# One layer of long convolution and routed experts: routing's small operations between the large ones, PSUM banks by user, the spectrum in two layouts

## The chip, the cores and the metric

The kernel runs on one core of a Trainium2 chip. The metric is the device time of one execution in microseconds (us): 2072.83 us as the median of three runs (2069.47 to 2073.29).

The engines are written as in the profile: PE is TensorE's matmul, PEld its weight load, DVE is VectorE, ACT ScalarE, POOL GpSimd, and SP the queue that issues most DMAs.

## The reference

```python
def _attn_ref(x, v, pos_emb, w1, w2):            # x, v: 4 x 11456 x 128
    h_mlp = np.maximum(pos_emb @ w1, 0.0) @ w2
    h_filt = h_mlp * np.exp(-0.01 * np.arange(S))[:, None]
    u = x * v
    Uf, Hf = np.fft.rfft(u, n=2*S, axis=1), np.fft.rfft(h_filt, n=2*S, axis=0)
    y = np.fft.irfft(Uf * Hf[None], n=2*S, axis=1)[:, :S, :]
    return x * y
def _moe_ref(x, modality_id, w_gate, modality_bias, w1, w2):   # 45824 rows, 8 experts
    logits = x @ w_gate + modality_bias[modality_id]
    e_idx = np.argmax(logits, axis=1)            # the gate is its softmax value
    for e in range(8):
        mask = e_idx == e
        out[mask] = gate_w[mask, None] * (np.maximum(x[mask] @ w1[e], 0) @ w2[e])
```

All of it is float32. A row of the convolution's output goes to one of eight experts, and the result goes back to the row's own place.

## The kernel before

**Convolution.** The transform of a batch is done as 90 x 64: a transform over 90 by matmuls with a constant matrix, then one over 64 that is folded into the second set of matmuls. The spectrum of a batch stays in SBUF in one tile `A` of 128 x 2 x 90 x 128 floats (block, frequency, channel).

Four kinds of stages follow each other on a written time line (`Timeline`, line 151). Each stage puts functions at times. `run` sorts them by time, place, rank and index, and this order is the program order of every engine, for the tile framework reorders nothing on PE, ACT, DVE and SP. Dependencies between instructions are kept by semaphores. For PSUM they are kept by whole banks within one tensor.

- The first stage builds the filter and transforms batch 0.
- A *middle* stage (`middle_stages`, line 546) has 23 groups. A group reads four frequencies of `A` (`spectrum`, 16 PE instructions at line 625), multiplies them by the filter's spectrum on DVE (lines 634, 643 and 652 or 654) and POOL, and transforms them back into `A` (`inverse`, line 669, copied by ACT at line 673).
- An *outer* stage (`outer`, line 849) has 16 steps `t` with some more for the routing's end. Outer stages 1 to 3 finish batch `b - 1` and start batch `b` in the same tile `A`. In a step:
  - `turn` (line 690) transposes a piece of `A` on PE: 16 transposes of a 128 x 90 operand with a 128 x 128 identity, in four banks, copied by four ACT copies.
  - `inverse_stages.transform` (line 697) makes the output `py` from these copies (line 703); ACT copies one half (706), DVE adds (707), subtracts (708) and multiplies by x, which is the *gate* (709).
  - `forward_stages` multiplies x and v on DVE (480), adds (483) and subtracts (484) the halves, and transforms the product of the step before on PE (495), copied by ACT into `A` (498).
  - `route_stages` works on octets `o`, one in two steps: two `turn` halves (751), `logits` (759), `logits_turn` (766), `biased` (772), `choice` with nine DVE operations (780 to 802), `send` with three matmuls `pr` (818 to 823) and four DVE operations (825 to 829), and `store`, the DMA of the finished rows (809), for which there are three `xo` tiles.
- The last outer stage, which has no next batch, has an order of its own (`LAST`). An expert stage follows it: 90 tiles of 512 rows, and some of 256.

The table `OUTER` (line 58) gives each function's step relative to its piece. `choice:3` runs at `t = q + 3`, where only odd `q` act; `send:4` comes one step after it. So the choice of an octet and its `pr` matmuls never stand in the same step. Even steps of an outer stage hold a choice, odd steps a send.

**PSUM.** There is a pool of four one-bank tiles (`bank`, line 200), which `turn`, routing and the middle's `pw` share, and a pool of two two-bank tiles (`pair`, line 374), which the forward transform, `py` and the middle's spectrum share.

Of the kernel before, what the change touches and what calls it, by code (L numbers as in the profile page):

```python
# [12 lines left out]
F32 = mybir.dt.float32  # L13
F32R = mybir.dt.float32r
BF16 = mybir.dt.bfloat16
# [23 lines left out]
NM = (NP + 1) // 2  # L39
NQ = N2 // 4  # L40
# [55 lines left out]
def shape_constants():  # L96
# [4 lines left out]
    fwd = np.zeros((2, 64, 2, N1))  # L101
    fwd[:, :HALF, 0], fwd[:, :HALF, 1] = even, odd
# [31 lines left out]
    tri = np.concatenate([-(q >= p).astype(float), np.ones((D, D))], 1)  # L134
# [10 lines left out]
        "c_fwd": f(fwd.reshape(D, 2 * N1)),   # L145
# [29 lines left out]
for _name, _n in (("tok", NC), ("first", E * NC), ("keep", E * NC),  # L175
                  ("tri", D), ("ones", D), ("reg", E), ("iota", NF)):
    SMALL[_name] = (_at, _at + _n)
    _at += _n
# [4 lines left out]
def hyena_moe_kernel(ctx: ExitStack, tc: tile.TileContext, a: dict, out: bass.AP,  # L183
# [16 lines left out]
    def bank(name):  # L200
        return banks[-1].tile([D, 512], F32, tag="ps", name=name)
# [13 lines left out]
    both = cst.tile([D, 2 * D], BF16, name="both")  # L215
# [152 lines left out]
    with ExitStack() as cv:  # L368
        banks.append(cv.enter_context(tc.tile_pool(name="ps", bufs=4, space=PSUM)))
        pairs = cv.enter_context(tc.tile_pool(name="pp", bufs=2, space=PSUM))  # L370
        keepp = cv.enter_context(tc.tile_pool(name="keepp", bufs=1))
        U = 1024

        def pair(name):
            return pairs.tile([D, 2, 512], F32, tag="pp", name=name)
# [3 lines left out]
        fwd = keepp.tile([D, 2, N1], F32, name="fwd")  # L379
# [24 lines left out]
        def split_constants():  # L404
            dve.tensor_scalar_add(base, sm("reg"), FAR)
            dve.tensor_copy(both, small[:, SMALL["tri"][0]:SMALL["ones"][1]])
# [16 lines left out]
        flatA = A.rearrange("p b k d -> p (b k d)")  # L423
# [43 lines left out]
        def forward_stages(b):  # L467
# [9 lines left out]
            def product(q):  # L477

                u, e = kept.pop((q, "xd")), kept.pop((q, "v"))
                paced(dve.tensor_mul(u, u, e))  # L480
                e = kept[q, "e"] = e.rearrange("p (c m) -> p c m", c=2)
                u = u.rearrange("p (w m) -> p w m", w=2)
                dve.tensor_add(e[:, 0], u[:, 0], u[:, 1])
                paced(dve.tensor_sub(e[:, 1], u[:, 0], u[:, 1]))

            def transform(q):

                e = kept.pop((q, "e")).rearrange("p c (j n) -> p c j n", n=N2)
                for h in range(2):
                    p = pair("s1")  # L490
                    for j in range(4):
                        for c in range(2):
                            for blk in range(2):
                                at = slice(64 * blk, 64 * blk + 64)
                                pe.matmul(p[64 * c:64 * c + 64, blk, N1 * j:N1 * j + N1],
                                          e[at, c, 4 * h + j], fwd[at, c], start=True, stop=True)
                    d0 = 8 * q + 4 * h
                    act.copy(A[:, :, :, d0:d0 + 4],
                             p[:, :, 0:4 * N1].rearrange("p b (n k) -> p b k n", n=4))
# [766 lines left out]
```

## Time and profile before

| | before |
|---|---|
| median of three runs | 2072.83 us |
| the profiled execution's own time | 2074.09 us |
| span in its profile | 2072.3 us |
| busy PE / PEld / DVE / ACT / POOL | 94% / 75% / 85% / 62% / 56% |
| mean granted TensorE clock | 0.982 of 2.4 GHz |
| DMA | 379.46 MB, 183 GB/s on the mean |

The shares are means over stages with different limits, so the page's first part can't be read as a bound. The order in which to read is: the stages (a window for each), then the instructions of one step in order of time, engine by engine. In a time line a row is a start, a length, an engine, a line and an operation; what stands in square brackets is the idle time before it and what ended it. An instruction may start before the one ahead of it has ended.

### The profile page before, as it was taken

What the parts mean: (1) busy time and instruction counts of PE and PEld (TensorE: products, weight loads), DVE (VectorE), ACT (ScalarE), POOL (GpSimd) and SP (SyncE); (2) the same over time, 40 slices, a digit from 0 to 9 for tenths busy, and PEclk for the clock granted to TensorE, in tenths of its full rate; (3) what the DMA queues carried; (4) which work ended last, traced back from release to release, by engine and by line L of the source; (5) the groups of instructions that cost most, each with busy time, mean ns of one, the idle gap of its engine ahead of it and who ended that gap; (6) DMA issues with size and microseconds to landing.
All of it is one profiled execution on the core that took longest, in us unless ns stands there. A gap on an engine that the chain in (4) does not pass through costs nothing. (4 is left out here: it accounts for less than half of the span.)

```text
span 2072.3 us, 50243 instructions
## 1 busy us (share of the span) xinstructions
PE 1958.3 (94%) x17646; PEld 1554.1 (75%) x17646; DVE 1752.4 (85%) x2612; ACT 1284.4 (62%) x2404; POOL 1169.4 (56%) x1054
## 2 busy tenths in 40 slices
PE   8899898999989998999789999999999999999997
PEld 8688665776667665776468888877888888888897
DVE  6599899999999899996678888897888778878886
ACT  5555675457744675456456666666666666666675
POOL 0144004766678476974456678786555555555654
PEclk9999999999999999999899999999999999999998
DMA  8565688889988898856787456654645555555421
GB/s 319 184 191 173 231 280 268 268 264 314 327 270 253 280 339 288 283 183 179 199 248 205 97 127 138 133 124 103 118 97 97 97 100 98 96 98 100 86 40 29
DMA packets 610842, 379.46 MB, mean 183 GB/s; under 512 B 424026, under 2 KB 542005, under 8 KB 610585
## 3 DMA queue, kind: packets, MB, share of 16 engines
q1 hardware_dynamic: 587193, 328.61, 58.2%
q0 software_dynamic: 23104, 47.34, 6.6%
q8 instruction: 141, 2.31, 0.5%
q14 instruction: 116, 0.95, 0.2%
q10 hardware_dynamic: 288, 0.25, 0.1%
HBM read 272.74 MB, written 103.70 MB: 182 GB/s over the span
## 5 line engine op out<-in xcount | busy, mean ns | idle before, releaser
L1094 ACT ACTIVATE hh<-ph 128x512 fp32r<-128x512 f32 x724 | 434.0, 599 | 323.2 <-PE ph L1091 320.2
L1095 DVE SCALAR_TENSOR_TENSOR hl<-ph,hh 128x512 fp32r<-128x512 f32 x724 | 488.5, 680 | 164.4 <-ACT hh L1094 155.6
L276 POOL DMA_INDIRECT xs<-back,to x360 | 405.4, 1126 | 319.9 <-DVE se L797 107.9
L1160 POOL DMA_INDIRECT out<-ot,x x362 | 373.3, 1031 | 160.2 <-issue 36.7
L1089 PE MATMUL ph<-xh,wh 128*128 128x512 f32 (+1 forms) x792 | 298.0, 376 | 8.3 <-ACT wh L1060 8.3
L1091 PE MATMUL ph<-xl,wh 128*128 128x512 f32 (+1 forms) x792 | 296.2, 374 | 9.0 <-POOL xl L1077 9.0
L1115 PE MATMUL po<-hl,wh 128*128 128x512 f32 (+1 forms) x792 | 295.6, 373 | 0.9 <-DVE hl L1095 0.6
L1090 PE MATMUL ph<-xh,wl 128*128 128x512 f32 (+1 forms) x792 | 295.6, 373 | 0.0
L1113 PE MATMUL po<-hh,wh 128*128 128x512 f32 (+1 forms) x792 | 295.1, 373 | 0.2 <-ACT hh L1094 0.2
L1114 PE MATMUL po<-hh,wl 128*128 128x512 f32 (+1 forms) x792 | 294.7, 372 | 0.0
L673 ACT COPY A<-pw 128x512 f32<-128x512 f32 (+1 forms) x184 | 97.1, 580 | 188.1 <-PE pw L669 188.1
L1077 POOL TENSOR_TENSOR xl<-xT,xh 128x512 fp32r<-128x512 f32 (+1 forms) x77 | 96.2, 1250 | 203.2 <-ACT xh L1073 203.2
L669 PEld LDWEIGHTS pw<-work 64*128 64x128 f32 x2856 | 167.2, 189 | 32.1 <-ACT work L607 19.2
L625 PE MATMUL pz<-A,work 128*64 128x256 f32 x1440 | 181.1, 394 | 8.3 <-DMA work<-in_c_to 5.0
L638 POOL TENSOR_TENSOR work<-work 128x512 f32<-128x512 f32 (+1 forms) x92 | 115.3, 1253 | 129.0 <-DVE work L634 128.4
L669 PE MATMUL pw<-work 64*128 64x128 f32 x2856 | 181.6, 279 | 4.7 <-POOL work L655 4.3
L1091 PEld LDWEIGHTS ph<-xl,wh 128*128 128x128 f32 x792 | 150.5, 190 | 37.0 <-POOL xl L1077 10.8
L1089 PEld LDWEIGHTS ph<-xh,wh 128*128 128x128 f32 x792 | 150.5, 190 | 33.6 <-ACT wh L1060 8.5
L1115 PEld LDWEIGHTS po<-hl,wh 128*128 128x128 f32 x792 | 150.0, 189 | 29.8 <-DVE hl L1095 4.2
L1090 PEld LDWEIGHTS ph<-xh,wl 128*128 128x128 f32 x792 | 150.6, 190 | 26.1 <-DVE wl L1061 0.4
L1113 PEld LDWEIGHTS po<-hh,wh 128*128 128x128 f32 x792 | 150.0, 189 | 26.1 <-ACT hh L1094 0.7
L1114 PEld LDWEIGHTS po<-hh,wl 128*128 128x128 f32 x792 | 150.0, 189 | 25.7
(181 smaller groups left out, 3613.9 us busy)
## 6 DMA issues: line engine op xcount, KB each, us to landing
work<-hs SPq DMA_DIRECT2D x66, 512.0 KB
work<-in_x SPq DMA_DIRECT2D x64, 512.0 KB
work<-in_xd SPq DMA_DIRECT2D x58, 512.0 KB
work<-in_v SPq DMA_DIRECT2D x51, 512.0 KB
xr<-xo SPq DMA_DIRECT2D x64, 365.6 KB
back<-xr SPq DMA_DIRECT2D x120, 195.0 KB
work<-in_c_to SPq DMA_DIRECT2D x88, 256.0 KB
blocks<-xs SPq DMA_DIRECT2D x328, 64.0 KB
```

Of the source, the lines that this page charges most:

```text
L276: s = pool.indirect_dma_start(out=xs, out_offset=bass.IndirectOffsetOnAxis(ap=ix, axis=0), in_=src, in_offset=None, bounds_check=E * R - 1 ...
L625: pe.matmul(z[64 * s:64 * s + 64, t, r], k["b"][:, t, s, r], A[:, :, 4 * g + 2 * t + s], start=True, stop=True)
L669: pe.matmul(v[s][:, t, blk], k[of][at, t, r, blk], k["c"][at, t, r], start=i == 0, stop=i == len(terms) - 1)
L1089: pe.matmul(p, k[0, "h"][:, f:f + D], k["xh"], start=True, stop=False)
L1090: pe.matmul(p, k[0, "l"][:, f:f + D], k["xh"], start=False, stop=False)
L1091: pe.matmul(p, k[0, "h"][:, f:f + D], k["xl"], start=False, stop=True)
L1094: act.activation(hh, ph, AF.Relu)
L1095: steps.append(ins_of(dve.scalar_tensor_tensor(hl, ph, 0.0, hh.bitcast(F32), op0=ALU.max, op1=ALU.subtract)))
L1113: pe.matmul(po, k[1, "h"][:, f], hh[:, t], start=g == 0, stop=False)
L1114: pe.matmul(po, k[1, "l"][:, f], hh[:, t], start=False, stop=False)
L1115: pe.matmul(po, k[1, "h"][:, f], hl[:, t], start=False, stop=g == NCH - 1)
L1160: s = pool.indirect_dma_start(out=out, out_offset=bass.IndirectOffsetOnAxis(ap=ix, axis=0), in_=src, in_offset=None, bounds_check=N - 1, o ...
```

## The change

- In `outer`, stages 1 to 3 no longer put their functions one by one. A function `step(t)` issues them in a written order. `product`, the inverse transform, `choice` and `send` are cut into lists of single DVE operations, and the routing's are put between the large ones. `choice` is spread over two steps: the maximum and the difference in the even step, the rest in the odd step after it. The three `pr` matmuls are issued at the end of this odd step, and the four DVE operations of `send` in the even step after that.
- One tile `psum` of eight banks takes the place of both pools. In stages 1 to 3 `turn` and the forward transform alternate between banks 4-5 and 6-7, `py` has 0-1, routing's turn, `logits` and `logits_turn` use bank 2, the other half of routing's turn and `pr` share bank 3. In the last outer stage `wt` and `xT` use banks 4 to 7.
- `A` holds the forward spectrum and the inverse's results in two layouts, `A_fwd` and `A_inv`, in the same places. The 90 frequencies are padded to 92. The spectrum's matmuls read runs of 8 floats (runs of 128 before). `inverse`'s copies write runs of 2 floats (128 before). `turn` loads columns 2 floats apart (128 before).
- `turn` and routing's `turn` go as two row tiles, partitions 0 to 63 and 64 to 127, into two banks. Their transposes are twice as many with a moving operand of 64 (or 45) columns. Two ACT copies take the place of four in `turn`. In the last outer stage both stay as they were.
- The constants for `pr` come as bfloat16 from the host, so one cast is gone.

```diff
-        A = keepp.tile([D, 2, N1, D], F32, name="A")
+        A = keepp.tile([D, 2 * NQ, 8 * KP], F32, name="A")
+        A_fwd = A.rearrange("p (b q) (j g n) -> p b q j g n", b=2, j=4, n=8)
+        A_inv = A.rearrange("p (b q) (h k i) -> p b (q h) k i", b=2, h=4, i=2)
...
+        def upper(name):
+            at = 4 + 2 * next_of("upper", 2)
+            return psum[:, at:at + 2]
...
-                                      A[:, :, 4 * g + 2 * t + s], start=True, stop=True)
+                                      A_fwd[:, :, :, 2 * t + s, g], start=True, stop=True)
...
-                    act.copy(A[:, :, k1:k1 + 2 * n - 1:2].rearrange("p b t m -> p t b m"),
-                             v[s][:, 0:n])
+                    act.copy(A_inv[:, :, :, k1:k1 + 2 * n - 1:2].rearrange("p b m t i -> p t (b m) i"),
+                             v[s][:, 0:n].rearrange("p t b (m i) -> p t (b m) i", i=2))
...
             def turn(q, blk):
+                if b == nb - 1:
...
+                    return
+                p = upper("wt")[0:N1].rearrange("p t (c j n) -> p t c j n", c=2, j=4)
                 for c in range(2):
-                    p = bank("wt")
                     for j in range(4):
-                        pe.transpose(p[0:N1, D * j:D * j + D], A[:, blk, :, 8 * q + 2 * j + c], ident)
-                    act.copy(w_t[q % 2][blk][:, c], p[0:N1])
+                        for t in range(2):
+                            at = slice(64 * t, 64 * t + 64)
+                            pe.transpose(p[:, t, c, j], A_inv[at, blk, 4 * q + j, 0:N1, c], ident[at, at])
+                act.copy(w_t[q % 2][blk].rearrange("p c (j t n) -> p t (c j) n", j=4, t=2),
+                         p.rearrange("p t c j n -> p t (c j) n"))
...
-                py = pair("py")
+                py = psum[:, 0:2]
...
-                pr = bank("pr")
+                if banks[-1] is single:
+                    pr = psum[:, 3, 512 - E * NC - E:512]
+                else:
+                    pr = bank("pr")
...
+            def step(t):
+                o, odd = t // 2 - 2, t % 2
+                here = 0 <= o < NO
+                if t < NQ:
+                    turn(t, 0)
+                    turn(t, 1)
+                if 0 <= t - 2 < NQ:
+                    rturn((t - 2) // 2, t % 2)
+                if here and odd:
+                    chosen["exp"]()
+                    chosen["tok"]()
+                if 0 <= t - 1 < NQ:
+                    transform(t - 1)
+                if here and not odd:
+                    lturn(o)
+                p = psteps(t) if 2 <= t < NQ else [lambda: None] * 3
+                c = lambda *names: [chosen[n]() for n in names] if here and odd else None
+                r = lambda k: sums.pop(k)() if k in sums and not odd else None
+                p[0](), c("sco", "se"), r(0)
+                p[1](), c("mb", "sum"), r(1)
+                p[2](), c("oh", "inv", "sc"), r(2)
+                if here and not odd:
+                    biased(o)
+                    chosen.update(csteps(o))
+                i = isteps(t) if t < NQ else [lambda: None] * 3
+                e = lambda name: chosen[name]() if here and not odd else None
+                i[0](), e("mx")
+                i[1](), e("dl")
+                i[2](), r(3)
+                if odd and 0 <= (t - 3) // 2 < NO and t >= 3:
+                    logits((t - 3) // 2)
+                if here and odd:
+                    sums.update(enumerate(ssteps(o)))
...
```

Here `rturn` is routing's turn, `transform` the forward one, `psteps` the product's three operations, `isteps(t)` issues the `py` matmuls and the ACT copy and returns the add, the subtract and the gate, `csteps` is the choice, and `ssteps(o)` issues the three `pr` matmuls and returns the four DVE operations `r`.

## Rows read from the trace of the kernel before

**Rows 1.** Windows by stage: length, busy PE PEld DVE ACT POOL, clock, DMA share, GB/s.

```profile
220.00:338.00 118.00, 112.63 (x1651) 77.00 (x1648) 108.98 (x195) 86.60 (x167) 7.99 (x8) 0.99 0.74 251
...
452.00:570.00 118.00, 110.39 (x1642) 75.35 (x1642) 106.66 (x191) 85.78 (x165) 71.97 (x60) 1.00 0.92 313
570.00:682.00 112.00, 104.48 (x1327) 81.30 (x1324) 106.03 (x96) 51.26 (x95) 84.91 (x72) 0.97 0.85 267
```

**Rows 2.** Time line of DVE, one even and one odd step of outer stage 2.

```profile
493.70 1.21 DVE L480 TENSOR_TENSOR work<-work 128x1024 f32<-128x1024 f32 x1
...
495.55 0.68 DVE L484 TENSOR_TENSOR work<-work 128x512 f32<-128x512 f32 x1
496.15 0.36 DVE L780 TENSOR_REDUCE mx<-lg 109x16 f32<-109x128 f32 x1
...
499.12 0.63 DVE L707 TENSOR_TENSOR work<-py,work 128x512 f32<-128x512 f32 x1
499.79 0.69 DVE L708 TENSOR_TENSOR work<-py,work 128x512 f32<-128x512 f32 x1
500.51 1.23 DVE L709 TENSOR_TENSOR xo<-work 128x1024 f32<-128x1024 f32 x1
501.65 1.22 DVE L480 TENSOR_TENSOR work<-work 128x1024 f32<-128x1024 f32 x1
...
503.52 0.68 DVE L484 TENSOR_TENSOR work<-work 128x512 f32<-128x512 f32 x1
504.30 0.69 DVE L707 TENSOR_TENSOR work<-py,work 128x512 f32<-128x512 f32 x1
...
507.61 0.38 DVE L829 TENSOR_REDUCE ix<-ro 109x16 int32<-109x128 f32 x1
...
508.10 1.21 DVE L480 TENSOR_TENSOR work<-work 128x1024 f32<-128x1024 f32 x1
```

**Rows 3.** Time line of PE, the even step that follows.

```profile
504.44 0.23 PE L818 MATMUL pr<-oh,both 109*128 109x128 bf16 x1
...
504.59 2.11 PE L694 MATMUL wt<-ident,A 128*90 128x128 f32 x16
506.54 0.68 PE L766 MATMUL lt<-ident,work 128*109 128x128 f32 x4
507.05 1.03 PE L751 MATMUL xT<-ident,xo 109*128 109x109 f32 x8
508.01 1.47 PE L495 MATMUL s<-fwd,work 64*64 64x90 f32 x64
509.74 1.94 PE L703 MATMUL py<-work,inv 90*64 90x512 f32 x8 [0.26 <-ACT A L498]
```

**Rows 4.** Time line of ACT in the same steps.

```profile
500.89 1.42 ACT L498 COPY A<-s 128x720 f32<-128x720 f32 x2
503.68 0.59 ACT L706 COPY work<-py 128x512 f32<-128x512 f32 x1 [1.38 <-PE py L703]
...
505.35 2.08 ACT L695 COPY work<-wt 90x512 f32<-90x512 f32 x4 [0.20 <-ACT work L761]
```

**Rows 5.** Time line of SP's DMA issues, the odd step.

```profile
504.14 1.77 SPq L809 DMA_DIRECT2D xr<-xo  x2
```

**Rows 6.** Waits in outer stage 2: us in total, times, longest.

```profile
DVE xo L709 <- DMA xr<-xo: 0.7, 1, 0.7
```

**Rows 7.** Time line of PE, one group of middle stage 2.

```profile
620.55 1.95 PE L625 MATMUL pz<-A,work 128*64 128x256 f32 x16
622.43 2.95 PE L669 MATMUL pw<-work 64*128 64x128 f32 x48
```

**Rows 8.** Time line of PE where outer stage 2 passes into the middle.

```profile
580.24 0.29 PE L818 MATMUL pr<-oh,both 109*128 109x128 bf16 x1 [4.99 <-DVE oh L790]
...
580.90 3.68 PE L625 MATMUL pz<-A,work 128*64 128x256 f32 x16
```

**Rows 9.** Window of the seven us around it, columns as in Rows 1.

```profile
580.00:587.00 7.00, 6.59 (x47) 4.44 (x49) 6.79 (x12) 1.86 (x4) 4.53 (x4) 0.55 0.77 235
```

More of the change, by code (lines that the diff above doesn't have):

```diff
@@ L39 @@
 NM = (NP + 1) // 2
+KP = 4 * NM
 NQ = N2 // 4
@@ L100, in shape_constants @@
     even, odd = np.cos(phi) + np.sin(phi), np.cos(phi) - np.sin(phi)
-    fwd = np.zeros((2, 64, 2, N1))
-    fwd[:, :HALF, 0], fwd[:, :HALF, 1] = even, odd
+    fwd = np.zeros((2, 64, 2, KP))
+    fwd[:, :HALF, 0, :N1], fwd[:, :HALF, 1, :N1] = even, odd
     whole = np.zeros((2, 64, 2, N1))
@@ L200, in bank @@
     def bank(name):
+        if callable(banks[-1]):
+            return banks[-1](name)
         return banks[-1].tile([D, 512], F32, tag="ps", name=name)
@@ L775, in choice, with choice_steps @@
             def choice(o):
+                steps = choice_steps(o)
+                for name in ("mx", "dl", "exp", "sco", "mb", "oh", "sc", "se", "tok", "sum", "inv"):
+                    steps[name]()
+            def choice_steps(o):
                 i = b * NO + o
@@ L839, in places @@
                         ix[64 * blk:64 * blk + HALF].rearrange("p (w m) -> p w m", w=2))
-            return turn, logits, logits_turn, biased, choice, send, store, places
+            return turn, logits, logits_turn, biased, choice, send, store, places, choice_steps, send_steps
         def every_other(f):
@@ L853, in outer @@
             if b > 0:
-                load_x, turn, itransform = inverse_stages(b - 1)
-                rturn, logits, lturn, biased, choice, send, store, places = route_stages(b - 1)
+                load_x, turn, itransform, isteps = inverse_stages(b - 1)
+                (rturn, logits, lturn, biased, choice, send, store, places,
+                 csteps, ssteps) = route_stages(b - 1)
                 todo = {
@@ L862, in outer @@
             if b < nb:
-                load, product, transform = forward_stages(b)
+                load, product, transform, psteps = forward_stages(b)
                 todo |= {"load": load, "product": product, "forward": transform}
@@ L874, in when @@
                 return ahead[i] if i < len(ahead) else min(i + d, TAIL) if b < nb else i + d
-            line.stages(at, NQ, LAST if b == nb else OUTER, todo,
-                        lambda name: 2 if name in LATE else 0, when)
+            if b == nb:
+                line.stages(at, NQ, LAST, todo, lambda name: 2 if name in LATE else 0, when)
+                return
+            line.stages(at, NQ, OUTER, {n: todo[n] for n in LATE}, lambda name: 2, when)
+            line.put(at - 2, lambda: product(0))
+            line.put(at - 1, lambda: product(1))
+            chosen, sums = {}, {}
+            def step(t):
[31 more added lines that the diff above has]
+                    sums.update(enumerate(ssteps(o)))
+                    if t > NQ:
+                        for k in range(4):
+                            sums.pop(k)()
+            for t in range(TAIL + 1):
+                line.put(at + t, lambda t=t: step(t))
         scratch = []
@@ L894, in hyena_moe_kernel @@
         todo = filter_stages()
-        load, todo["product"], todo["forward"] = forward_stages(0)
+        load, todo["product"], todo["forward"], _ = forward_stages(0)
         for name in ("xd", "v"):
```

166 lines of the change are left out of this document (103 added, 63 removed).

## The prediction, made before the change was run

> **What bounds the kernel now.** I read the windows first [rows 1]. Experts, after 1030 us, are not touched by the change. In outer stages 1 to 3 DVE is busy for 109 and 107 of 118 us and PE for 113 and 110, so neither is ruled out, and the mean over a stage mixes steps with and without routing. So I went on to the time lines of one even and one odd step. On DVE [rows 2] the distance of the two rows L480, 493.70 and 508.10, is 14.40 us, and DVE has next to no idle time in it. On PE in the same place [rows 3] the py matmuls come after an idle 0.26 us, and ACT shows gaps of up to 1.38 us [rows 4]. So a step with routing is bound by DVE, and an early step, without choice and send, by PE: 1.95 (wt) + 0.96 (xT) + 1.73 (s) + 1.87 (py) = 6.5 us, from start to start in rows 3 and a little under its length for py.
>
> The reader is to see something finer in rows 2. L780, which doesn't need the result of the instruction before it, starts at 496.15, 0.08 us before that one ends (495.55 + 0.68). L708, which needs L707's work, starts at 499.79, 0.04 us after its end (499.12 + 0.63). An instruction that depends on its predecessor thus starts 0.12 us later than one that does not. This is all that dealing the operations out can win on DVE.
>
> In the middle PE has no gap: 1.95 us at L625 and 2.95 at L669 make up a group [rows 7]. Where an outer stage passes into the middle, PE stands still for 4.99 us behind a `pr` that waits for the choice; the granted clock is 0.55 in the window, so the lower level is in force, and L625 takes 3.68 us instead of 1.95 [rows 8, 9].
>
> **The change, part by part.**
>
> *Dealing out.* By the code a pair of steps has 15 DVE instructions that follow directly on the one they need: L480 to 483 twice, 707 to 708 and 708 to 709 twice each, five in the choice up to `sc`, two up to the reciprocal, 825 to 826 and 827 to 829. Two are left afterwards, the odd step's add, subtract and gate. 13 x 0.12 = 1.55 us: DVE alone could do a pair in 14.40 - 1.55 = 12.85 us.
>
> *The new wait.* It will not get all of that. The second half of the choice and its `pr` matmuls now stand in the same odd step, `pr` as the last thing on PE. Behind `pr` in PE's order are the turn, routing's turn, the forward transform, `lt` and `py` of the even step, and the add L707 of that step needs `py` and its copy. So two legs follow each other in every pair.
> DVE's leg, from the even step's L707 to `sc` in the odd step: L707 to the gate's end, 501.65 - 499.12 = 2.53, less 2 x 0.12 = 2.29; the choice's nine operations, 499.12 - 496.15 = 2.97, less 7 x 0.12 = 2.13; the product, 496.15 - 493.70 = 2.45 less 0.12 = 2.33; L829, 0.38 [rows 2]. Together 7.13.
> PE's leg, from `sc` to that L707: 0.07 us until `pr` starts (three such hand-overs are 0.14 in all, by 0.04 as above and a little more to PE), `pr` 0.15 (504.44 to 504.59), the turn, routing's turn, the forward transform 1.47, `lt` 0.51, `py` 1.94 [rows 3], the copy 0.59 [rows 4]. Turns as two row tiles are not in the trace. Below, half of today's 1.95 and 0.96; above, no gain. The nearest row is `s`, whose tiles of 64 x 64 run four together: 64 of them in 1.47 are 0.092 us for four with 90 columns, 0.065 with 64. 16 pairs are 1.04 us, routing's 8 pairs 0.52. The two turns now use two bank pairs in turn with the forward transform, with one large copy each: half of 2.08, 1.04 [rows 4]. The first copy ends 0.52 + 0.04 + 1.04 = 1.60 after the turn's start, the second 2.64; the second half of the forward transform would come at 1.04 + 0.52 + 0.73 = 2.29 and waits some 0.38. Sum: 0.14 + 0.15 + 1.04 + 0.52 + 0.38 + 1.47 + 0.51 + 1.94 + 0.59 = 6.74 (bounds 6.6 and 7.7). The cycle is 7.13 + 6.74 = 13.87, or -0.53 us a pair, and with five whole pairs -2.6 us a stage. DVE, late no more by its own work, will wait for `y` once in a pair.
>
> *Early steps.* 1.04 + 0.52 + 0.38 + 1.47 + 1.94 = 5.35 instead of 6.5, -1.15; three such steps make -3.4 us a stage.
>
> *The end of the stage gives back.* The last choice and `pr` come a group later than now and the whole written step is one lump before the middle's next function. PE's 4.99 us of idle time becomes about twice as long, and the low clock after it lasts into one more L625 or L669. At the full clock +1.1 us (the early-step gain lost again), with a further low group 3.68 - 1.95 = 1.7 and the wait's own growth, up to 5. I take 3.2, the middle of it.
>
> *Edits at nothing.* 92 instead of 90 columns: 2% of 1.47, in the sum's rounding. The forward copies have 736 elements instead of 720 in 1.42, before ACT's idle 1.38 [rows 4]. `inverse`'s copies write runs of two floats: ACT is busy for 51 of 112 us in the middle [rows 1], which covers up to twice their length. The cast that goes stood in the first stage, before DVE was the bound: 0 to -0.3. The last outer stage keeps its order: 0, bounds of ±2 us for the new banks. `store` now waits for a reciprocal that comes 1.2 us later in its step (at 3.7 instead of 2.5 us; the issue was at 504.14 [rows 5]). Behind it in SP's order stand the loads, which are asked for earlier than needed, and the gate, which waits for a free `xo`, waited 0.7 us in the whole stage [rows 6]: taken as 0, bound 1.2 x 5 octets x 3 stages = +18. The DMA share of 0.92 in outer stage 2 [rows 1] also says that this stage can't get under 118 x 0.92 = 109 us.
> The spectrum's matmuls read runs of 8 floats. In the trace they read only whole runs of 128. The nearest rows are those of the turns: `wt` takes its weights from A at a stride of 128 floats and costs 1.95 / 16 = 0.122 us an instruction, `xT` takes them in whole runs and costs 0.96 / 8 = 0.120 [rows 3]. That is 2%, or 0.04 us for each of 92 groups, +4. A moving operand may differ from weights; as the far end I set, for want of any row, a quarter of L625's 1.95, 0.49 x 92 = +45. I take 0, by the 2%. The Trainium skill (SBUF — State Buffer, "Door 1: The DMA port swizzle") gives lines of 16 bytes, of which a run of 8 floats is two whole ones; that would be no cost. No row here shows it.
>
> *Sum.* -3.4 - 2.6 + 3.2 = -2.8 us for a stage, -8.4 for three. The profiled execution took 2074.1 us, so 2065.7; it lies 1.3 above the median of the runs, so 2064 there.
>
> **The rivals** (all on the median's side).
> DVE stays the bound and gets all of it: PE's leg would have to be under 12.85 - 7.13 = 5.7. Then 5.5 pairs x 1.55 = -8.5, and -3.4 + 3.2 as above, -8.7 a stage, 2047. For it: `pr` might be passed early, as the clock of rows 8 is not the rule. Against it: the matmuls alone are 5.6. 15%.
> Slower, by one mechanism: PE's leg gets longer than 14.40 - 7.13 = 7.27. If row tiles bring nothing, it is 6.74 - 1.56 - 0.38 + 1.95 + 0.96 = 7.71, the cycle 14.84, +2.2 us a stage, no early gain, and the end's +3.2 to +5: +5.4 to +7.2 a stage, 2089 to 2094. For it: each transposition has its own weight load, and twice as many are issued. 19%.
> The spectrum's short runs slow L625 by up to a quarter: 2064 + 45 = 2109. 4%.
> The end of each stage eats all that the steps give, or `store`'s delay does: 2072. For it speaks row 8's 4.99 us. 22%.
> An instruction starts only when the one before has left the pipe, dependent or not, and dealing out wins nothing: DVE's leg 7.13 + 9 x 0.12 = 8.2, the cycle 14.95, +2.8 a stage and +3.2 - 3.4, some +8 in all with the late `store`, 2081. The Trainium skill says so (VectorE: DVE Perf Modes, "The DRAIN you can't avoid"): each instruction waits until the pipeline is empty. By that rule the trace disagrees: 0.08 before the end against 0.04 behind it [rows 2]. 2%.
>
> **How the numbers follow.** The forecast holds 38%, with its own range of 2056 to 2072. A measurement of this kernel tells 0.2%, some 4.1 us, from no change. Faster: 30 of the forecast's 38, and the 15 of the rival that gets all, 45%. Same: 8 + 22 = 30%. Slower: 19 + 4 + 2 = 25%. The range that leaves out 2 in 10 reaches from the full gain, 2047, to the slower rival's middle, 2092.
>
> **What would show it.** Right: the distance of two even steps' L480 is 13.9 us; `pr` waits for DVE's `sc` once a pair, and L707 of the even step waits for ACT's copy; early steps take 5.4; L625's 16 instructions take 1.95 in the middle; the wait before the middle is longer than 4.99. Wrong: 12.9 us without a DVE gap (the first rival), wt's 32 instructions still taking some 1.95 (the second), L625 over 2.1 (the third), a gate that waits for a DMA of `xr` in each octet.

## The result, and the profile after

The changed kernel takes 2093.64 us (median of 4), the kernel before 2071.15 beside it: ratio 1.011, 95% interval 1.0089 to 1.0131. Forecast was a faster kernel, 2064 us in a range of 2047 to 2092. The changed kernel is slower than the one before by 22 us and lies above the range. It lies within the slower rival's 2089 to 2094, but not by that rival's mechanism, as will be seen.

Where the time went can be read by stages. The table is made from the starts of `py` and of the spectrum's matmuls in each profiled execution (an outer stage from its first `py` to the first spectrum group, a middle from there to the next `py`); the three columns on the right belong to kernels of the experiments below.

| us | before | after | late_ix | r3_early | final |
|---|---|---|---|---|---|
| first stage, middle 0 | 224.4 | 225.2 | 225.3 | 225.9 | 225.4 |
| outer 1 | 113.8 | 115.5 | 116.0 | 114.5 | 109.5 |
| middle 1 | 115.1 | 118.5 | 112.3 | 116.8 | 114.4 |
| outer 2 | 117.5 | 120.8 | 124.4 | 113.8 | 112.5 |
| middle 2 | 113.0 | 117.3 | 112.5 | 118.3 | 114.9 |
| outer 3 | 117.9 | 122.4 | 125.5 | 115.8 | 116.1 |
| middle 3 | 118.5 | 124.1 | 118.5 | 121.5 | 121.9 |
| last outer | 109.5 | 111.5 | 110.5 | 111.1 | 109.8 |
| experts | 1042.6 | 1039.2 | 1043.4 | 1043.0 | 1041.3 |

From before to after, the three outer stages lose 9.5 us, the three middles 13.3, the last outer stage 2.0, the start 0.8, and the experts give 3.4 back: 22.2.

The windows of after that answer to [rows 1], with the columns of those rows:

```profile
225.20:340.70 115.50, 105.08 (x2001) 67.58 (x2001) 98.69 (x192) 82.92 (x134) 10.49 (x10) 0.97 0.76 252
459.20:580.00 120.80, 106.67 (x2003) 69.91 (x2003) 99.47 (x191) 83.27 (x134) 64.77 (x60) 0.96 0.89 300
580.00:697.30 117.30, 105.55 (x1353) 82.04 (x1351) 106.36 (x94) 53.15 (x96) 84.90 (x73) 0.96 0.82 261
```

DVE's busy time in an outer stage has fallen to 99 us of 121. No engine is busy for the whole of the stage any more, so the bound must be a wait. PE's instructions are 2003 instead of 1642, in fewer busy us.

Three pairs of steps in outer stage 2, same columns:

```profile
495.80:510.10 14.30, 13.06 (x271) 8.57 (x266) 12.76 (x28) 10.51 (x18) 8.88 (x9) 1.00 0.90 265
510.10:526.80 16.70, 12.91 (x248) 8.48 (x241) 12.70 (x27) 10.30 (x18) 8.72 (x9) 0.95 0.88 317
526.80:543.10 16.30, 14.06 (x263) 9.64 (x261) 12.83 (x28) 10.67 (x18) 8.85 (x9) 0.92 0.87 292
```

The first takes 14.21 us by its L508 rows below, near the forecast 13.87. Those behind it take 16.2 to 16.8 us from L508 to L508, with the same DVE work. DVE's time line of the first two, answering to [rows 2] (L508 is the product's multiplication, L753 the inverse's add, L749 the gate, L859 `sc`, L903 `ix`):

```profile
495.85 1.22 DVE L508 TENSOR_TENSOR work<-work 128x1024 f32<-128x1024 f32 x1
...
500.50 0.69 DVE L753 TENSOR_TENSOR work<-psum,work 128x512 f32<-128x512 f32 x1 [1.08 <-ACT work L745]
...
507.13 0.45 DVE L859 TENSOR_TENSOR_SCAN sc<-small,oh 109x128 bf16<-109x128 f32 x1
...
510.06 1.22 DVE L508 TENSOR_TENSOR work<-work 128x1024 f32<-128x1024 f32 x1
...
514.71 0.69 DVE L753 TENSOR_TENSOR work<-psum,work 128x512 f32<-128x512 f32 x1 [1.08 <-ACT work L745]
...
518.95 1.23 DVE L749 TENSOR_TENSOR xo<-work 128x1024 f32<-128x1024 f32 x1 [2.47 <-DMA xr<-xo]
520.09 0.37 DVE L903 TENSOR_REDUCE ix<-ro 109x16 int32<-109x128 f32 x1
...
526.83 1.22 DVE L508 TENSOR_TENSOR work<-work 128x1024 f32<-128x1024 f32 x1
...
535.19 1.23 DVE L749 TENSOR_TENSOR xo<-work 128x1024 f32<-128x1024 f32 x1 [0.95 <-DMA xr<-xo]
```

In the second pair the gate at 518.95 waits 2.47 us for a store of `xo`. In the kernel before such waits made 0.7 us in a whole stage [rows 6]. The reason stands in SP's queue, the DMA issues in order of time (answering to [rows 5]; L912 issues `places`, L874 the store):

```profile
508.13 1.76 SPq L874 DMA_DIRECT2D xr<-xo  x2
...
514.72 0.33 SPq L496 DMA_DIRECT2D work<-in_v  x1
520.49 1.76 SPq L912 DMA_DIRECT2D xi<-ix  x2
522.42 0.43 SPq L262 DMA_DIRECT2D back<-xr  x1
522.91 0.41 SPq L713 DMA_DIRECT2D work<-in_x  x1
523.37 0.43 SPq L496 DMA_DIRECT2D work<-in_xd  x1
523.89 0.38 SPq L496 DMA_DIRECT2D work<-in_v  x1
524.38 1.76 SPq L874 DMA_DIRECT2D xr<-xo  x2
```

`places` is issued 0.03 us after `ix` ends (520.09 + 0.37), and for 5.4 us before it, from 515.05, the queue issues nothing. `ix` now stands behind the gate. In the kernel before it ended at 507.99 [rows 2], and its `places` (L837 there) went out 4.4 us later, behind three loads:

```profile
512.39 2.38 SPq L837 DMA_DIRECT2D xi<-ix  x2
```

In the changed kernel a read back, three loads and the next store come behind `places` in the queue; the store goes out 3.9 us after it, and that store's landing is what the gate after next waits for. So gate, `ix`, `places`, loads and store have become a ring: from the gate 1.5 us to `places`, 3.9 to the store, and 10.8 to the gate after next, at 535.19: 16.2 us. The store has a second late operand, the reciprocal, which ends at 523.99, only 0.39 us before the store goes out. So this trace alone doesn't tell which of the two makes the ring. SP's waits in outer stage 2, us in total, times, longest; first after, then before:

```profile
SPq L912 <- DVE ix L903: 17.6, 4, 5.4
```

```profile
SPq L837 <- DVE xo L802: 1.7, 2, 1.3
SPq L837 <- DVE work L707: 1.5, 1, 1.5
```

PE's time line of the same pairs, answering to [rows 3] (L890 is `pr`, L728 the turn, L807 routing's turn, L521 the forward transform, L822 `lt`, L742 `py`):

```profile
507.11 0.22 PE L890 MATMUL psum<-oh,small 109*128 109x128 bf16 x1 [0.84 <-DVE oh L857]
...
507.80 1.56 PE L728 MATMUL psum<-ident,A 64*90 64x64 f32 x32
509.20 0.66 PE L807 MATMUL psum<-ident,xo 64*128 64x64 f32 x16
509.79 1.77 PE L521 MATMUL psum<-fwd,work 64*64 64x92 f32 x64
511.49 0.69 PE L822 MATMUL psum<-ident,work 128*109 128x128 f32 x4
512.11 1.94 PE L742 MATMUL psum<-work,inv 90*64 90x512 f32 x8
...
523.87 0.22 PE L890 MATMUL psum<-oh,small 109*128 109x128 bf16 x1 [3.39 <-DVE oh L857]
...
524.56 1.81 PE L728 MATMUL psum<-ident,A 64*90 64x64 f32 x32
```

A late gate makes DVE's next step late, so `pr` keeps PE standing for 3.39 us instead of 0.84, and the turn behind it takes 1.81 instead of 1.56: the granted clock falls to its lower level for a part of each such pair (0.95 and 0.92 in the windows above).

The passage into the middle, PE, answering to [rows 8] (L650 is the spectrum):

```profile
579.97 1.95 PE L650 MATMUL psum<-A,work 128*64 128x256 f32 x16
581.85 0.69 PE L822 MATMUL psum<-ident,work 128*109 128x128 f32 x4
586.96 3.44 PE L650 MATMUL psum<-A,work 128*64 128x256 f32 x16 [4.42 <-DVE lg L828]
596.34 0.26 PE L890 MATMUL psum<-oh,small 109*128 109x128 bf16 x1 [5.94 <-DVE oh L857]
...
597.00 3.54 PE L650 MATMUL psum<-A,work 128*64 128x256 f32 x16
...
602.45 1.95 PE L650 MATMUL psum<-A,work 128*64 128x256 f32 x16
```

PE stands still twice, 4.42 and 5.94 us, where it did so once for 4.99 [rows 8], and two groups take 3.44 and 3.54 us instead of 1.95, at the lower clock (0.64 granted from 596 to 602 us). From the first group to the fourth it is 22.5 us here and 16.6 before (570.8 to 587.4). The 1.95 us of the last row shows that the spectrum's runs of 8 floats cost nothing at the upper clock ([rows 7]).

### The profile page after: what moved, and what is told of

It is laid out like the page before. It is cut to its first block, busy times and chain, and to the rows that moved or that the text cites. A ratio compares the mean times of both kernels' runs of the same rounds, so it can differ in the third digit from the quotient of the medians.

```text
span 2094.5 us, 52194 instructions
## 1 busy us (share of the span) xinstructions
PE 1947.8 (93%) x18798; PEld 1535.2 (73%) x18798; DVE 1723.9 (82%) x2611; ACT 1283.4 (61%) x2308; POOL 1148.8 (55%) x1054
## 5 line engine op out<-in xcount | busy, mean ns | idle before, releaser
L280 POOL DMA_INDIRECT xs<-back,to x360 | 385.2, 1070 | 338.2 <-DMA back<-xr 115.9
L698 ACT COPY A<-psum 128x512 f32<-128x512 f32 (+1 forms) x184 | 106.4, 639 | 202.4 <-PE psum L694 202.4
L650 PE MATMUL psum<-A,work 128*64 128x256 f32 x1440 | 187.5, 405 | 9.2 <-DVE lg L828 4.4
L694 PEld LDWEIGHTS psum<-work 64*128 64x128 f32 x2856 | 165.3, 188 | 28.6 <-ACT work L632 20.0
L694 PE MATMUL psum<-work 64*128 64x128 f32 x2856 | 178.6, 277 | 2.4 <-POOL work L680 2.1
```

The lines of the kernel that those rows point to most:

```text
L280: s = pool.indirect_dma_start(out=xs, out_offset=bass.IndirectOffsetOnAxis(ap=ix, axis=0), in_=src, in_offset=None, bounds_check=E * R - 1 ...
L650: pe.matmul(z[64 * s:64 * s + 64, t, r], k["b"][:, t, s, r], A_fwd[:, :, :, 2 * t + s, g], start=True, stop=True)
L694: pe.matmul(v[s][:, t, blk], k[of][at, t, r, blk], k["c"][at, t, r], start=i == 0, stop=i == len(terms) - 1)
```

## The experiments

Three theories. **P**: PE's wait for `pr`, with the low clock behind it, sets the pair. **S**: the store comes late because its reciprocal does. **Q** (formed after the second group): the store comes late because `places` blocks SP's queue until `ix` is there. For the passage **B**: the banks of the last octet's `lt` and `pr`. A ratio is to the kernel before in the same group of runs.

### First group: every kernel took longer

In this group the kernel before took 2123 us; on the same chip it took 2074 us in the fifth group. The changed kernel was not among the runs, so no ratio here is compared with one of another group.

**early_inv**, a changed order in the odd step:

```diff
-                p[0](), c("sco", "se"), r(0)
-                p[1](), c("mb", "sum"), r(1)
-                p[2](), c("oh", "inv", "sc"), r(2)
+                p[0](), c("se", "sco", "sum", "inv"), r(0)
+                p[1](), c("mb"), r(1)
+                p[2](), c("oh", "sc"), r(2)
```

> Order of the odd step's small DVE operations changed: the sum of exponentials, its 1e-9 and the reciprocal come right behind the product's first operation, about 1.75 us earlier; sc, which pr waits for, comes 0.12 us later. Theory S (the store loop: gate, 5.0 us to the reciprocal, store, some 10.3 us to its landing, next gate but one into the same xo tile; 16.3 us a pair in outer stages 2 and 3): the pairs there fall from 16.3-16.7 to about 14.5 us, 8 or 9 pairs, about -14 to -16 us, 2078. Theory P (PE standing still for pr, and the low clock after it, set the pair): pr comes no earlier, so the pairs stay at 16.3 us and the time at 2094 or a little above.

**pr_later**:

```diff
+                if not odd and 0 <= o - 1 and t <= NQ:
+                    sums.update(enumerate(ssteps(o - 1)))
                 if here and not odd:
                     lturn(o)
...
-                if here and odd:
+                if here and odd and t > NQ:
                     sums.update(enumerate(ssteps(o)))
```

> The three pr matmuls are issued in the even step behind the forward transform instead of at the end of the odd step; nothing else moves. Theory P: PE no longer stands still in front of a turn, the clock stays at its upper level, and pairs go to DVE's 12.9 us in all stages: about -40 us, 2053. Theory S: only pairs without a store wait win (14.2 to 13, about 9 of them, mostly in outer stage 1), the others stay near 16 us: -8 to -12 us, 2083.

**junction**:

```diff
+                tail = t >= NQ
-                if here and odd:
+                if here and odd and not tail:
                     chosen["exp"]()
...
+                if here and not odd and tail:
+                    r(3)
+                    for n in ("mx", "dl", "exp", "sco", "mb", "oh", "sc", "se", "tok", "sum", "inv"):
+                        chosen[n]()
```

> In the steps after the last piece (t >= 16) the choice is made whole in the even step, as in the kernel before, and pr follows a step later. Both theories: PE's second standstill in the passage to the middle (5.9 us before pr) goes, with one of two groups at the low clock, 6 to 9 us a passage; the middle gives some of it back, since loads that came in time behind a late start make it wait again (1.6 to 4.7 us). -9 to -20 us in all, 2074 to 2085; pairs of outer steps unchanged at 16.3 us.

**all3** is the three together.

> The three edits together: reciprocal early, pr a step later, last choices whole. Theory S: pairs in outer stages 2 and 3 at the shortened store loop of 14.4 us, in stage 1 at 12.9; early_inv's -15, junction's -9 to -20 and a little of pr_later: 2055 to 2068, at or below the kernel before. Theory P: 12.9 us everywhere, about 2040 to 2045.

Measured: 2157.86 (1.0176, interval 1.0147 to 1.0205), 2180.40 (1.0272, 1.0233 to 1.0311), 2161.15 (1.0198, 1.0147 to 1.0248) and 2153.36 us (1.015, 1.012 to 1.0179). Routing's pairs in outer stage 2 took 16 to 21 us, and the trace of junction shows a part of why: PE pauses inside one line's instructions, and nothing in the trace releases it. The forward transform's rows have 33 to 58 such pauses in each of the four traces, and at most 3 in after, after_2, r3_early and final.

```profile
502.86 0.38 PE L521 MATMUL psum<-fwd,work 64*64 64x92 f32 x5 [0.55 <-issue]
503.45 0.41 PE L521 MATMUL psum<-fwd,work 64*64 64x92 f32 x5 [0.21 <-issue]
...
504.96 2.87 PE L521 MATMUL psum<-fwd,work 64*64 64x92 f32 x51 [0.42 <-issue]
```

The 64 matmuls take 5.0 us instead of 1.77. What this is stays open, and the group tells no theory apart. pr_later and junction were not run again by themselves.

### Second group: the reciprocal is not the cause

**after_2** is the changed kernel again.

> The changed kernel itself again, beside the others of this group and the kernel before. Where the chip is like the one of the first result: ratio 1.011, pairs of outer stages 2 and 3 at 16.3 to 16.7 us. On the chip of the first group of experiments, where the kernel before took 2123 us: above early_inv's 1.018 by theory S, equal to it by theory P.

**early_inv_2** and **all3_2** are the kernels from above.

> The reciprocal 1.75 us earlier, as before, now beside the changed kernel. Theory S: 14 to 16 us under it, pairs in outer stages 2 and 3 at 14.5 us. Theory P: the same as it.

> The three edits on the changed kernel again (reciprocal early, pr a step later, last choices whole). Theory S: pairs of outer stages 2 and 3 at 14.4 us, of stage 1 at 12.9, one standstill less in each passage to the middle: 25 to 40 us under the changed kernel, at or below the kernel before. Theory P: 12.9 us everywhere, 50 us under it.

**late_recip** puts the late reciprocal into the kernel before:

```diff
+                if late and q % 2:
+                    late.pop()()
                 s = dve.tensor_mul(xo_of(b, q // 2)[:, :, q % 2, :, 0:D], four(y),
...
-                paced(dve.reciprocal(xov[:, :, :, D], by_h(se)))
+                late.append(lambda: paced(dve.reciprocal(xov[:, :, :, D], by_h(se))))
+                if b == nb - 1 or 2 * o + 5 >= NQ:
+                    late.pop()()
```

> The kernel before with one edit: the reciprocal of an octet, and so its store, comes in the odd step between the subtract and the gate, some 6 us later than now; the choice, pr, turns and spectrum stay as they were. Theory S: gate to reciprocal's end 505.7 - 500.5 = 5.3 us, store and landing 10.5, gate 0.7: pairs in outer stages 2 and 3 go from 14.3 to about 16.4 us, stage 1, whose stores land some 2 us faster, little; 9 to 10 pairs, +15 to +20 us. Theory P: pr and PE see nothing of it, 0 to +2 us.

Measured: after_2 2099.86 (1.0123, 1.0103 to 1.0142); early_inv_2 2103.52 (1.015, 1.0129 to 1.0172), no gain; late_recip 2073.57 (1.0011, 0.9998 to 1.0024), its pairs with routing at 14.1 to 15.0 us (14.3 to 14.9 before). Theory S falls on both sides. all3_2: 2088.48 (1.0066, 1.0046 to 1.0086), half of what was lost; with `pr` moved, PE waits for `pr` no more in outer stage 2, yet pairs of stages 2 and 3 still take 13.2 to 17.5 us, so P is not the cause either. What after_2, early_inv_2 and all3_2 have in common is SP's wait for `ix`, 18.2, 16.0 and 14.2 us between 460 and 570 us, which none of the edits touched.

### Third group: `ix` and the queue

**late_ix** moves one operation of the kernel before behind the gate, and gives its operand `ro` a buffer of its own, since it is now read later:

```diff
                 s = dve.tensor_mul(xo_of(b, q // 2)[:, :, q % 2, :, 0:D], four(y),
                                    four(kept.pop(q)))
+                if late and q % 2 == 0:
+                    late.pop()()
...
-                ro = rt.tile([PU, E, NC], F32, tag="ex", name="ro", bufs=1)
+                ro = rt.tile([PU, E, NC], F32, tag="ro", name="ro", bufs=1)
...
-                dve.tensor_reduce(ix[0:PU].rearrange("p (g h) -> p h g", h=4),
-                                  ro.rearrange("p e (h g) -> p h g e", h=4), axis=AX.X, op=ALU.min)
+                late.append(lambda: dve.tensor_reduce(
+                    ix[0:PU].rearrange("p (g h) -> p h g", h=4),
+                    ro.rearrange("p e (h g) -> p h g e", h=4), axis=AX.X, op=ALU.min))
+                if b == nb - 1 or 2 * o + 6 >= NQ:
+                    late.pop()()
```

> The kernel before with one edit: the last of send's four DVE operations, ix, comes behind the gate of the even step that follows, as in the changed kernel; choice, pr, turns, spectrum and banks stay as they were. Theory Q: the pairs of outer stages 2 and 3 go from 14.3 to about 16.4 us and the time up by 12 to 20 us, 2085 to 2092; stage 1, where landing takes 7 to 8 us, changes little. Rivals P and S: 0 to +2 us.

Measured: 2092.32 (1.0105, 1.008 to 1.013), about the loss of the whole change. In the table its outer stages 2 and 3 take 6.9 and 7.6 us more than before, while outer 1 and the middles change by -2.8 to +2.2. SP's and DVE's waits in its outer stage 2 (L843 is `places`, L709 the gate):

```profile
SPq L843 <- DVE ix L832: 18.8, 5, 6.4
```

```profile
DVE xo L709 <- DMA xr<-xo: 7.4, 3, 3.2
```

So a late `ix` alone makes a loss of this size, without bank plan, row tiles, layouts or dealing out. It makes it in the outer stages; the 13.3 us that the middles lose in after are not in it.

**places_later**:

```diff
-         "inverse:0 logits:2 send:4 load_x:-1 load:-2 store:4 places:5")
+         "inverse:0 logits:2 send:4 load_x:-1 load:-2 store:4 places:6")
```

> One number of the changed kernel: the DMA that writes the places (xi from ix) is issued one step later, so that it stands behind ix's reduction by a whole step and doesn't wait in SP's queue. Theory Q (SP's queue: gate, ix's reduction behind it, then places, one or two reads back, three loads and the next store in SP's order, 3.9 us from places to store; 10.5 us to landing, 0.5 to the gate; 16.5 to 16.9 us a pair): the pairs of outer stages 2 and 3 fall from 16.4 to 14.2 to 14.7 us, 9 pairs, -14 to -20 us against the changed kernel: 2078 to 2085. Rivals: theory P (PE's wait for pr and the low clock after it) no change, 2094 to 2100; theory S (the reciprocal) no change.

**places_junction** adds junction's edit to it, **all4** adds pr_later's and early_inv's too.

> Places later, and the last two choices whole in the even step as in the kernel before. Theory Q with the junction's own loss: the second of PE's two standstills in each passage goes, 5 us and a group at the low clock, of which the middle takes back 2 to 4: 10 to 18 us under places_later alone, 2063 to 2072.

> Places later, last choices whole, pr a step later and the reciprocal early. PE's leg behind pr is gone, so nothing but DVE's work is left for a pair: 12.9 to 13.3 us where DMA allows it (a share of 0.92 at 14.7 us a pair says 13.5 at least in stages 2 and 3). 0.7 to 1.2 us x 15 pairs under places_junction: 2050 to 2062, 0.5 to 1% under the kernel before.

Measured: 2101.56 (1.013, 1.0096 to 1.0165), 2091.51 (1.0093, 1.0072 to 1.0114), 2078.19 (1.0034, 1.0018 to 1.0051), all three above what Q forecast. In places_later the first two pairs of routing in outer stage 2 are back at 14.2 and 14.5 us (the third still takes 16.7) and no gate waits for `xr`, but the time did not follow. Two new waits of its outer stage 2, SP's and DVE's:

```profile
SPq L267 <- DMA xi<-ix: 2.0, 1, 2.0
```

```profile
DVE xo L749 <- DMA work<-in_x: 5.6, 2, 3.2
```

The fetch at L267 reads what `places` wrote, and it now waits in the queue for it, ahead of the loads; and gates wait for a load of x. Some loss had only moved within SP's queue, and the middles, at 120.3 to 127.4 us against 117.3 to 124.1 in after, got longer too.

### Fourth group: banks, dealing out, row tiles

**tail_banks**:

```diff
-                pt = kept[o] = psum[:, 2]
+                pt = kept[o] = psum[:, 6 if o == NO - 1 and not last else 2]
...
-                    pr = psum[:, 3, 512 - E * NC - E:512]
+                    pr = psum[:, 7 if o == NO - 1 and not last else 3, 512 - E * NC - E:512]
```

> The changed kernel with two banks changed: lt of the last octet of an outer stage in bank 6 and its pr in bank 7, instead of 2 and 3. Theory B (the middle's second spectrum group, in banks 2 and 3, waits until DVE has read lt there, behind the first group's products): the second group starts 2.5 to 3.5 us after the first instead of 7 to 8.4; 4 us a passage, of which the middle's loads take back 1 to 2: -6 to -12 us against the changed kernel, 2083 to 2090. Rival: the late choice alone holds PE up, the second group's gain is lost again before pr, and the time stays at 2094 to 2100.

Measured: 2094.06 (1.0088, 1.0064 to 1.0112). PE in its passage:

```profile
579.46 1.95 PE L650 MATMUL psum<-A,work 128*64 128x256 f32 x16
...
581.96 1.95 PE L650 MATMUL psum<-A,work 128*64 128x256 f32 x16
593.53 0.27 PE L890 MATMUL psum<-oh,small 109*128 109x128 bf16 x1 [9.62 <-DVE oh L857]
```

B holds for the first standstill: the second group comes after 2.5 us, as in the kernel before. But the wait for `pr` grows from 5.94 to 9.62 us, so that from the first group to the fourth it is 21.3 us instead of 22.5. The two standstills had one end, DVE's late choice; a time gain against the changed kernel is not clear of its interval.

**best** is the changed kernel with early_inv, junction, both bank edits (`pr` of the last two octets in bank 7), places at 6, `pr` in the even step to the end, and

```diff
-                line.put(at + 13, lambda b=b: fetch(2 * b - 2), 3)
+                line.put(at + 15, lambda b=b: fetch(2 * b - 2), 3)
```

**best_dense** takes the dealing out back out of it, **best_full** the turns' row tiles:

```diff
-                p[0](), c("se", "sco", "sum", "inv"), r(0)
-                p[1](), c("mb"), r(1)
-                p[2](), c("oh", "sc"), r(2)
+                p[0](), p[1](), p[2]()
+                c("sco", "mb", "oh", "sc", "se", "sum", "inv")
+                r(0), r(1), r(2)
...
-                        for t in range(2):
-                            at = slice(64 * t, 64 * t + 64)
-                            pe.transpose(p[:, t, c, j], A_inv[at, blk, 4 * q + j, 0:N1, c], ident[at, at])
+                        pe.transpose(p[:, c, D * j:D * j + D], A_inv[:, blk, 4 * q + j, 0:N1, c], ident)
```

> The changed kernel with all that the runs pointed to: places a step later and the fetch that reads them two steps later, the reciprocal early, pr a step later in all steps, the last two choices whole, lt and pr of the last octets in banks 6 and 7. If queue and banks are the whole loss: pairs at 12.9 us (13.5 where DMA is full), passages at 17 us to the fourth group as in the kernel before: 15 pairs x 1.0 to 1.4 us and 9 early steps x 1 us under the kernel before, 2045 to 2055. If something else holds, 2065 to 2078 as in all4.

> best with the dealing out undone: the same operations in the same steps, but product, choice, sums and inverse each in one piece, so that 13 instructions a pair start behind the one they need. If the 0.12 us a dependent start hold: 14.4 us a pair where DVE is the bound, +1.5 x some 15 pairs, +15 to +23 us against best. Rival (each start waits for an empty pipe anyhow): +0 to +3 us.

> best with the turns as 16 transposes of 128 rows a step instead of 32 of 64, into the same banks with the same copies; routing's turn stays as it is. PE's step gets 0.55 us longer (1.95 instead of 1.40). If DVE bounds the pairs, only the early steps, 9 x 0.55, show it: +3 to +6 us. If PE does: +1.1 us x 20 pairs, +15 to +22 us.

Measured: best 2095.84 (1.0106, 1.0089 to 1.0123), far above what was expected. Its first expert matmul comes at 1036.5 us of its profile (after: 1055.3), but the expert stage takes 1059.5 us instead of 1039.2. Windows in the experts of all4 and of best:

```profile
1397.00:1697.00 300.00, 297.61 (x1311) 245.43 (x1310) 240.23 (x383) 199.70 (x354) 176.91 (x170) 1.00 0.54 103
```

```profile
1400.00:1700.00 300.00, 282.23 (x1232) 232.05 (x1231) 230.95 (x364) 187.48 (x333) 174.88 (x166) 0.97 0.51 99
```

PE is idle for 18 us of the 300 in best, which it is not in all4. All three kernels with the later fetch have this longer stage (1058 to 1060), and outside the first group none of the others; that the fetch is its cause was not tried by itself.

best_dense: 2103.32 (1.0149, 1.0111 to 1.0188), some 7 us above best with intervals that overlap. Its pairs in outer stage 1 take 13.88 us. best_full: 2095.11 (1.0113, 1.0095 to 1.0132), the same as best. The row tiles of the turns save 0.25 us in an early step (5.6 instead of 5.85 in the traces), and nothing that the time shows.

### Fifth group: the one operation

**r3_early** moves one call of the changed kernel:

```diff
+                r(3)
                 i = isteps(t) if t < NQ else [lambda: None] * 3
...
-                i[2](), r(3)
+                i[2]()
```

> One operation of the changed kernel moved: ix's reduction stands before the inverse's add, not behind the gate, so the places DMA no longer waits for a gate. All DMAs stay in their steps. Theory Q: pairs of outer stages 2 and 3 at 14.2 to 14.6 us instead of 16.4 on the mean, 9 pairs, -14 to -18 us; the middle takes back a third of it, as it did in the other runs: 2080 to 2090. Rivals (PE's wait for pr and the clock; the reciprocal): 2092 to 2100.

Measured: 2079.47 (median of 12; 1.0028, 1.0014 to 1.0042). Outer stages 2 and 3 take 113.8 and 115.8 us, against 120.8 and 122.4. DVE's waits in its outer stage 2:

```profile
DVE work L753 <- ACT work L745: 9.2, 9, 1.9
...
DVE xo L749 <- DMA xr<-xo: 0.2, 1, 0.2
```

The wait for the store is gone but for 0.2 us, and `places` waits 2.4 us in the stage, in four rows of 0.4 to 0.8 and none of them for `ix`, instead of 17.6. That the place of `ix` is the cause is shown from both sides: late_ix brings the loss into the kernel before, r3_early takes most of it, 0.8 to 1.0% of the time, out of the changed one.

One part of theory Q the traces don't bear out: that the time at which the store goes out makes the loss. The table has one round of outer stage 2 in each run, from an even step's gate to the store and from there to the gate that writes the stored tile again.

| | gate, store, next gate, us | gate to store | store to next gate | read back to store |
|---|---|---|---|---|
| before | 529.62, 534.23, 544.65 | 4.61 | 10.42, waits 0.67 | 4.31 |
| after | 518.95, 524.38, 535.19 | 5.43 | 10.81, waits 0.95 | 1.96 |
| late_ix | 516.32, 521.90, 532.69 | 5.58 | 10.79, waits 2.36 | 2.11 |
| late_recip | 502.08, 507.64, 516.38 | 5.56 | 8.74, no wait | 5.06 |
| r3_early | 514.65, 520.50, 529.87 | 5.85 | 9.37, no wait | 5.37 |

In late_recip and r3_early the store goes out as late behind its gate as in after and late_ix, and nothing waits for it, for it lands sooner. So the time to the landing, no constant, decides the round together with that of the issue. In after and late_ix, where `places` has blocked the queue, the read back and the three loads go out within some 2 us ahead of the store, and in late_recip and r3_early over 5 (last column); but in the kernel before they take 4.3 and the store still lands late. So this crowding doesn't explain the landing by itself, and what does stays open. Of r3_early's round, SP's rows and the gate:

```profile
515.13 0.47 SPq L262 DMA_DIRECT2D back<-xr  x1
...
520.50 1.91 SPq L874 DMA_DIRECT2D xr<-xo  x2
```

```profile
529.87 1.21 DVE L749 TENSOR_TENSOR xo<-work 128x1024 f32<-128x1024 f32 x1
```

**final** is r3_early with early_inv, junction, the bank edits and `pr` a step later; places and fetch are where the change had them.

> r3_early with pr a step later, the reciprocal early, the last two choices whole, their lt and pr in banks 6 and 7; places and fetch in their old steps. If the queue, the wait for pr and the banks are the losses: convolution as in best, 1030 to 1036 us up to the first expert, and experts again at 1038 to 1042: 2068 to 2077, no clear difference from the kernel before, though a pair takes 12.9 to 13.6 us instead of 14.3, because the middle waits for loads instead.

Measured: 2067.38 (median of 12; 0.9972, 0.9954 to 0.9989), the only version faster than the kernel before, by 0.3%. DVE's L508 at the start and at the end of a pair of its outer stage 1:

```profile
271.04 1.21 DVE L508 TENSOR_TENSOR work<-work 128x1024 f32<-128x1024 f32 x1
...
283.96 1.21 DVE L508 TENSOR_TENSOR work<-work 128x1024 f32<-128x1024 f32 x1
```

This pair takes 12.92 us, with no wait of DVE's in it: the floor of 12.85 from the prediction, which the wait for `pr` hid in the change as it was. In outer stages 2 and 3, where the DMA share is 0.94, routing's pairs still take 13.0 to 15.8 us.

## Why the prediction was wrong

The step that failed is the one on the queue: "`store` now waits for a reciprocal that comes 1.2 us later in its step", with the loads behind it "asked for earlier than needed", "taken as 0". It followed the store and its reciprocal and never named `places`, the other DMA of routing, whose operand `ix` the change moves by half a pair and behind a gate. In its place the runs showed `places` holding up SP's queue, 17.6 us in outer stage 2, and gates that wait for stores behind it; `ix` ahead of the gate again was worth 17 to 20 us of the time (the ratios of after and after_2 against r3_early's). The bound of +18 put on the queue has that size, but for the wrong DMA, so its nearness is luck: late_recip, whose reciprocal is later still, cost 0 to 0.2%.

That is the greater part of the 30 us between forecast and measurement, not all of it. With `ix` back in time r3_early stands at 1.0028, 6 us above the kernel before, where 8 below were forecast, so the sum fails in the steps too. They were to win 6.0 us a stage. In r3_early the steps with routing and the early ones together (from the third L508 of a stage to the sixteenth) are 4.4, 2.9 and 2.0 us shorter than before.

Point by point:

- **Dealing out, 0.12 us a start.** The floor held: 12.92 measured in final, 12.85 forecast. Undoing it costs 13.88 - 12.92 = 0.96 us a pair by best_dense, not 1.55, though best_dense is not the old order in all.
- **The new wait for `pr`.** Right in mechanism and nearly in size: DVE's leg 500.50 to 507.58 is 7.08 us (7.13 forecast), PE's from there to 514.71 is 7.13 (6.74), the cycle 14.21 (13.87). PE's term was short at the turn, 1.40 from start to start against 1.04. The slower rival, which needed more than 7.27, did not come about: its time was right by another cause. In r3_early, whose `ix` is out of DVE's leg, the pairs of stage 1 behind the first take 13.87 us, against 14.30 before; those of stages 2 and 3 take 13.8 to 15.2, against 14.4 to 14.9, so little of the gain was left there. What holds them was not tried; the DMA share is 0.93.
- **Early steps.** Two of them take 5.6 us against 6.28 and 6.51 before; 5.35 instead of 6.5 was forecast. The third step that the prediction counted as early took 7.9 us before and takes 7.3.
- **The end of the stage gives back.** 3.2 us forecast; the middles of r3_early, without the ring, are 1.7, 5.3 and 3.0 longer than before. In after it is 3.4, 4.3 and 5.6. The two standstills cost 5.9 to 9.1 us up to the fourth group, so the middle takes part of it back; that its loads are then there in time is the likely reason, and not shown.
- **Edits at nothing.** The spectrum's short runs cost nothing (1.95 us). The gate's wait was looked for in the text as what would prove it wrong, "a gate that waits for a DMA of `xr` in each octet", and such waits are what the trace shows, in two of the gates between 459 and 580 us.
- **Left out.** The first stages and the last outer stage are 0.8 to 2.0 us longer; no run looked into it.

## What to carry to other kernels

When an operation is moved, list every DMA that reads its result, and what is queued behind that DMA on its issuing engine: in these runs a DMA that waited held up all later ones of its queue, needed or not. A queue that joins a consumer's wait to its own next store makes a ring, and its length, not any engine's busy time, is then the bound; such a ring is found by reading the issue times of one queue over two rounds. The time from a store's issue to its landing is no constant in it: read it in each run. And a wait that is removed from a queue by delaying its DMA can come back at that DMA's reader.

## What the runs showed of the hardware

- The turn's 32 instructions took 1.81 us instead of 1.56 right after PE had stood still for 3.39 us; in the pair before, 0.84 us of standing had no such price.
- Two row tiles halve neither turn: 1.40 us from start to start instead of 1.95, and 0.59 instead of 0.96.
- The time from the issue of the same store to the gate that writes its tile again was 10.4 to 10.8 us in rounds of before, after and late_ix, and at most 8.7 and 9.4 us in rounds of late_recip and r3_early, where no gate waited. Why stays open.
- On one occasion the three kernels that were also run at another time took 2.5 to 3.1% longer (before: 2123 us), with PE pausing 0.2 to 0.55 us between matmuls of one line in the traces taken then. Why stays open.
